# Attention and feed-forward on one core: the order of the two half-array scores after a row-maximum block

## The chip, the cores and the metric

The kernel runs on one core of a Trainium2 chip. The metric is device time of one execution in microseconds (us). The engines are named as in the profile: PE (TensorE matmuls), PEld (TensorE weight loads), DVE (VectorE), ACT (ScalarE), POOL (GpSimd) and SP (the queue that issues most DMAs).

## The reference

```python
def _attn_ref(q, k, v):                       # q, k, v: 4 x 8 heads x 1152 x 64
    factor = 2
    scale = 1.0 / np.sqrt(D)
    q_pool = q.reshape(B, H, S // factor, factor, D).mean(axis=3)
    scores = scale * np.matmul(q_pool, k.transpose(0, 1, 3, 2))
    scores = scores - np.max(scores, axis=-1, keepdims=True)
    attn = np.exp(scores)
    attn = attn / (np.sum(attn, axis=-1, keepdims=True) + 1e-09)
    return np.matmul(attn, v).astype(np.float32)

def _moe_ref(x, w_in, w_out, alpha):          # x: 2304 x 512, w_in: 512 x 2048
    h = x @ w_in
    g = np.maximum(h, 0.0) + alpha * np.minimum(h, 0.0)
    return (g @ w_out).astype(np.float32)
```

The attention output of all heads, laid side by side, is the x of the second function.

## The kernel before

The 32 heads are worked through in 16 pairs. A pair's two heads lie in the two halves of the 128 partitions, 64 dimensions each, so a matmul that contracts over one head's dimensions uses 64 rows of the array. The lower 64 rows are called tile 0 here and the upper 64 rows tile 1; a matmul on one can run beside a matmul on the other.

**Row maxima** (`pair_max`, `rows` at L818 and L825, `peaks` at L839). For a pair there are 28 row-maximum blocks, each of them for one head, so on one tile; in the list they alternate tile 0, tile 1. A block is one matmul of 384 columns (L818), or two of 288 columns (L825), into a PSUM bank, which DVE then reduces to a maximum for each row. The maxima reach the scores later as a fourth term (`mq`). The row maxima of pair n+1 are spread between the scores of pair n.

**Scores** (`half_main`, `scores` at L951). A pair has two halves of 288 query columns, and a half has 9 score blocks of 128 keys. A score block is 8 matmuls of 288 columns: four terms (high by high, high by low, low by high, and minus the maximum), each for tile 0 and then tile 1. Tile 0 accumulates in one PSUM bank and tile 1 in another. Two exponentials on ACT (L968) then read these banks, tile 0's first, and write `p`. In program order a block is tile 0, tile 1, tile 0, tile 1 and so on, whatever stood in front of it. I write S0 and S1 for the first score matmul of a block on tile 0 and on tile 1.

**The rest of a half.** POOL or DVE adds up the `p` tiles (L981); PE multiplies them by V (`weighted`, L995, 36 matmul records in a row for one half); the sums (L1017) give the denominators; DVE and ACT finish the rows (L1054 to L1066) and SP writes them to DRAM.

**Feed-forward** (L479). Low and high sweeps, three matmuls a product, use the whole array. From about 388 us on they are mixed into the last halves, and after 444 us PE does nothing else.

**What sets the order.** All of this is given to a planner (`Scheduler`) as tasks with priorities and estimated durations. It places one task after another on the engines and calls `emit` as it does so, and with that the order on each engine is fixed in the program. A score block is one task, and so is each exponential. PSUM banks are given out by the planner too. Each engine works its list from front to back and waits at semaphores.

Of the kernel before, what the change touches and what calls it, by code (L numbers as in the profile page):

```python
# [13 lines left out]
AF = mybir.ActivationFunctionType  # L14
# [15 lines left out]
class Buf:  # L30


    def __init__(self, ring=None):
        self.ring, self.t = ring, None
        self.writers, self.users = [], []
        if ring:
            ring.made.append(self)
# [71 lines left out]
class Scheduler:  # L109
# [3 lines left out]
    def __init__(self, col_cost, turn, to_pe, from_pe, slack, dma_fixed):  # L113
        self.tasks, self.ready = [], [[] for _ in range(5)]
        self.free = [0.0] * 5
        self.dma_free = 0.0
        self.now = 0.0
        self.col = 0
        self.lock_free = 0.0
        self.turn = turn  # L120
        self.col_cost, self.to_pe, self.from_pe, self.slack = col_cost, to_pe, from_pe, slack
        self.dma_fixed = dma_fixed
        self.hold = ()

    def add(self, eng, dur, emit, reads=(), writes=(), uses=(), deps=(), prio=0.0, col=0, size=0, kind=None, dma=False, lock=False, fixed=None):
        t = Task()
# [99 lines left out]
def attention_ffn(  # L226
# [87 lines left out]
    nc = tc.nc  # L314
# [6 lines left out]
    HQ = SQ // 2  # L321
# [6 lines left out]
    SCALE = 0.5 / float(D) ** 0.5  # L328

    def dve(n):  # L330
        return (n + 65) / 0.96

    def act(n, psum=False):
        return n / 1.2 + (50 if psum else 93)
# [14 lines left out]
    sch = Scheduler(COL, SF, TO_PE, FROM_PE, (SLP, SLA, SLD, 0, 0), DF)  # L349
# [285 lines left out]
    both = [slice(i * D, (i + 1) * D) for i in range(2)]  # L635
# [156 lines left out]
    def pair_max(n, w):  # L792
# [15 lines left out]
        for x, (t, j, i) in enumerate(items):  # L808
            ms, d = Buf(r_ms), both[i]
            p = n - M0 - 0.5 * MS * (len(items) - 1 - x)  # L810
            if first:
                p = -9 + 0.01 * x
            rest = t < 0
            m = S // 4 if rest else JW

            def rows(t=t, j=j, d=d, ms=ms):
                if t >= 0:
                    nc.tensor.matmul(  # L818
                        out=ms.t[:, :JW], lhsT=w.q1.t[d, starts[t]:starts[t] + P],
                        rhs=w.k1.t[d, j * JW:(j + 1) * JW], start=True, stop=True,  # L820
                    )
                    return
                for u in range(2):
                    c = (2 * j + u) * (S // 4)
                    nc.tensor.matmul(  # L825
                        out=ms.t[:, :S // 4], lhsT=w.rt.t[d, D - D * u:D - D * u + P],
                        rhs=w.k1.t[d, c:c + S // 4], start=u == 0, stop=u == 1,
                    )

            dur = 190 if rest else 130  # L830
            if first:
                deps = w.k_in if rest else [w.k_in[j], w.q_in[2 * (t > 1)]]
                add(PE, dur, rows, uses=[w.q1, w.k1], reads=[w.rt] if rest else (), deps=deps, writes=[ms], prio=p, kind="m", col=1)
            else:
                add(PE, dur, rows, reads=[w.rt if rest else w.q1, w.k1], writes=[ms], prio=p, kind="m", col=1)

            def peaks(t=t, j=j, i=i, ms=ms, m=m):
                at = i if t < 0 else 2 + t + i * (NQT - 1)
                nc.vector.tensor_reduce(out=bx.t[:, at, j:j + 1], in_=ms.t[:, :m], axis=AX.X, op=ALU.max)  # L839

            add(DVE, dve(m), peaks, reads=[ms], writes=[bx], prio=p)
            if first and x in (4 * NJ + 3, len(items) - 1):
                first_turn(x > 4 * NJ + 3, w, bx, mx, mq)
# [9 lines left out]
        def turn():  # L853
            for i, d in enumerate(both):
# [3 lines left out]
        t = [  # L858
            add(
                ACT, 110, lambda i=i, d=d: nc.scalar.activation(out=mm.t[:, d], in_=mt.t[i][:2 * NQT, :D], func=AF.Copy),  # L860
                reads=[mt], writes=[mm], prio=n - M0,
            )
            for i, d in enumerate(both)
        ]
# [3 lines left out]
                out=mm.t[:2, :D], in0=mt.t[1][:2, :D], in1=mm.t[:2, :D].bitcast(F32), op=ALU.max  # L868
# [3 lines left out]
        for i in range(2):  # L872
# [3 lines left out]
                    out=mq.t[i * D:i * D + 1, :REM].bitcast(F32).rearrange("o (t p) -> o t p", p=P),  # L876
                    in_=mm.t[2 + i * (NQT - 1):2 + (i + 1) * (NQT - 1)].bitcast(F32),
# [52 lines left out]
    def pair_main(n, w):  # L930
        for h in range(2):
            half_main(n, h, w)

    def half_main(n, h, w):
        late_head = n + h >= JH
        heads = [g[0] for g in PARTS[late_head]]
        ends = [g[-1] for g in PARTS[late_head]]
        acc[n + h], avs[n + h] = [], Buf(r_avs)
        av = Buf(r_av)
        t_acc, t_av, ps_ = None, None, []  # L940
        q = slice(h * HQ, (h + 1) * HQ)
        for c in range(NC):
            s = slice(c * P, (c + 1) * P)
            p, ps = Buf(r_p), Buf(r_ps)
            at = n + h + c / NC

            def scores(ps=ps, s=s):
                pairs = ((w.k1, w.q1), (w.k1, w.q2), (w.k2, w.q1), (None, w.mq))
                for x, (k, r) in enumerate(pairs):
                    for i, d in enumerate(both):  # L950
                        nc.tensor.matmul(  # L951
                            out=ps.t[i][:, :HQ], lhsT=k.t[d, s] if k else neg[d], rhs=r.t[d, q],
                            start=x == 0, stop=x == len(pairs) - 1,
                        )

            if n:
                add(PE, 545, scores, reads=[w.k1, w.q1, w.k2, w.q2, w.mq], writes=[ps], prio=at, kind="s", col=1)
            else:
                t = add(
                    PE, 545, scores, reads=[w.k1, w.q1, w.q2], uses=[w.k2, w.mq],  # L960
                    deps=w.k_low[:1 + (c >= 4)] + w.mq_in[0] + (w.mq_in[1] if h else []),
                    writes=[ps], prio=at, kind="s", col=1,
                )
                first_score.append(t)
            for i in range(2):
                add(
                    ACT, act(HQ, True),
                    lambda ps=ps, p=p, i=i: nc.scalar.activation(  # L968
                        out=p.t[:, i], in_=ps.t[i][:, :HQ], func=AF.Exp, scale=SCALE
                    ),  # L970
                    reads=[ps], writes=[p], prio=at + 0.01 * i,
                )
            if c in heads:

                part, t_acc, alone = p, None, True
            else:
                a, part = part, Buf(r_acc) if alone else part
                eng, dur, e = (DVE, dve(2 * HQ), nc.vector) if c in ADDS[late_head] else (POOL, 2.4 * 2 * HQ + 50, nc.gpsimd)
                t_acc = add(
                    eng, dur,  # L980
                    lambda a=a, b=p, part=part, e=e: e.tensor_tensor(out=part.t, in0=a.t, in1=b.t, op=ALU.add),  # L981
                    reads=[a, p], writes=[part], deps=[t_acc] if t_acc else [], prio=at, lock=True,
                )
                alone = False
            if c in ends:
                acc[n + h].append(part)
            ps_.append(p)
            if c not in GROUPS[late_head]:
                continue

            def weighted(c=c, ps_=ps_):
                for x, p in enumerate(ps_):
                    e = c - len(ps_) + 1 + x
                    for i in (1, 0):
                        nc.tensor.matmul(  # L995
                            out=av.t[i * D:(i + 1) * D, :HQ], lhsT=w.vv[i].t[:, e], rhs=p.t[:, i],
                            start=(e == 0), stop=(e == NC - 1),
                        )

            t_av = add(  # L1000
                PE, 486 * len(ps_), weighted, reads=w.vv + ps_, writes=[av],
                deps=[t_av] if t_av else [], prio=n + h + (c + GL) / NC, col=2,
            )
            ps_ = []
        add(
            ACT, act(HQ, True), lambda: nc.scalar.activation(out=avs[n + h].t, in_=av.t[:, :HQ], func=AF.Copy),
            reads=[av], writes=[avs[n + h]], prio=n + h + 1,
        )
# [70 lines left out]
    with ExitStack() as actx:  # L1079
# [64 lines left out]
        for n in range(0, NH, 2):  # L1144
# [4 lines left out]
        t = add(SP, 600, lambda: nc.sync.dma_start(out=nal, in_=alpha), uses=[], writes=[nal_b], deps=[first_load[0]], prio=3)  # L1149
# [3 lines left out]
                out=nal, in0=nal, scalar1=-1.0, scalar2=0.0, op0=ALU.mult, op1=ALU.add  # L1153
# [8 lines left out]
        for c in range(REUSE):  # L1162
            f, i = NLO + c // 2, c % 2
# [70 lines left out]
```

## Time and profile before

| what | value |
|---|---|
| device time, median of 3 runs | 840.44 us (839.09 to 842.27) |
| the profiled execution's own time | 839.95 us |
| span from its first to its last instruction | 838.2 us |
| PE busy | 825.2 us (98%) |
| DVE busy | 567.0 us (68%) |
| ACT busy | 437.4 us (52%) |
| mean granted TensorE clock | 0.999 |

A busy PE is not a PE at its peak: matmul records on the two tiles overlap, and a record is longer than the time until the next matmul on the same tile can start. A short wait between two matmuls therefore hides under the record of the one before.

### The profile page before, as it was taken

The numbers are of one execution on the slowest core, as the hardware profiler recorded it, in microseconds if no ns is written. First come the engines' busy times: TensorE is split into PE (matmuls) and PEld (weight loads), VectorE is DVE, ScalarE is ACT, GpSimd is POOL, SyncE is SP. The second block draws the span as 40 slices with busy tenths as digits, with TensorE's granted clock in tenths as the row PEclk, the third lists the DMA queues.
The fourth block names the chain that finished last, engine by engine and source line by source line (L and its number), as shares of the span: only waits on it lengthen the run. The fifth ranks groups of instructions, "written<-read, shape, count | busy, mean of one in ns | idle before, by whom it ended". The sixth has DMA issues, their size and how long they took to land.

```text
span 838.2 us, 17447 instructions
## 1 busy us (share of the span) xinstructions
PE 825.2 (98%) x6690; PEld 691.4 (82%) x6690; DVE 567.0 (68%) x1035; ACT 437.4 (52%) x1124; POOL 262.4 (31%) x196
## 2 busy tenths in 40 slices
PE   8999999999999999999999999999999999999997
PEld 8767777676777777776779999998898988988986
DVE  7999999999998988889963799632242232322422
ACT  4657676675766676665754676643232233332321
POOL 5665665565565665654550000000000000000000
PEclk9999999999999999999999999999999999999999
DMA  8234345634354433323233768581330421300301
GB/s 274 58 89 164 82 144 140 197 115 123 87 179 122 122 116 77 83 72 109 69 124 121 248 195 260 177 228 58 91 92 3 120 59 46 91 0 1 91 1 45
DMA packets 67759, 93.71 MB, mean 112 GB/s; under 512 B 20004, under 2 KB 45404, under 8 KB 67676
## 3 DMA queue, kind: packets, MB, share of 16 engines
q1 hardware_dynamic: 65516, 88.18, 33.9%
q0 software_dynamic: 2160, 4.42, 3.6%
q8 instruction: 52, 0.85, 0.4%
q14 instruction: 31, 0.25, 0.1%
HBM read 73.48 MB, written 19.02 MB: 110 GB/s over the span
## 4 chain that ended last, share of the span: by engine, by line
PE 86%; DVE 9%; DMA 2%; issue 1%; ACT 1%; SPq 0%; DVEq 0%; ACTq 0%
PE bank L479 44%; PE bank L951 18%; PE bank L995 15%; PE bank L818 6%; DVE bx L839 3%; PE bank L1017 2%; DMA wraw<-wt 1%; DVE x L1066 1%; DVE pa L981 1%; PE bank L825 1%; PE bank L1129 1%; DMA kk<-kt 1%; DVE pos L515 1%; DVE r L1054 0%; DVE wbits L415 0%
## 5 line engine op out<-in xcount | busy, mean ns | idle before, releaser
L981 POOL TENSOR_TENSOR pa<-pa,pa 128x576 f32<-128x576 f32 x160 | 240.5, 1520 | 155.9 <-ACT pa L968 104.4
L839 DVE TENSOR_REDUCE bx<-bank 128x1 f32<-128x384 f32 (+1 forms) x448 | 214.0, 533 | 22.5 <-PE bank L818 19.9
L968 ACT ACTIVATE pa<-bank 128x288 f32<-128x288 f32 x576 | 199.7, 417 | 25.9 <-PE bank L951 17.4
L951 PE MATMUL bank<-q,k 64*128 64x288 f32 x1728 | 206.2, 311 | 0.8 <-DVE mq L923 0.6
L951 PEld LDWEIGHTS bank<-q,k 64*128 64x128 f32 x1728 | 163.3, 184 | 21.1 <-issue 9.3
L995 PE MATMUL bank<-pa,vv 128*64 128x288 f32 x1152 | 146.8, 409 | 0.0
L995 PEld LDWEIGHTS bank<-pa,vv 128*64 128x64 f32 x1152 | 79.9, 137 | 54.8 <-issue 3.8
L526 DVE TENSOR_TENSOR gw<-gs,gw 128x460 fp32r<-128x460 f32 (+1 forms) x55 | 35.1, 638 | 121.2 <-ACT gw L521 121.2
L951 PE MATMUL bank<-mq,neg 64*128 64x288 f32 x576 | 115.2, 291 | 0.0
L818 PE MATMUL bank<-k,q 64*128 64x384 f32 x384 | 110.1, 362 | 3.5 <-DVE bx L839 2.0
L521 ACT ACTIVATE gw<-gs 128x460 fp32r<-128x460 f32 (+1 forms) x55 | 32.4, 589 | 126.7 <-PE bank L479 115.2
L479 PE MATMUL bank<-wlow,wh 128*128 128x460 f32 (+1 forms) x320 | 93.0, 371 | 0.0
L479 PE MATMUL bank<-gw,wh 128*128 128x460 f32 (+1 forms) x320 | 92.8, 371 | 0.0
L951 PEld LDWEIGHTS bank<-mq,neg 64*128 64x128 f32 x576 | 83.3, 184 | 0.0
L818 PEld LDWEIGHTS bank<-k,q 64*128 64x128 f32 x384 | 62.4, 185 | 16.2 <-DVE bx L839 10.0
L515 DVE SCALAR_TENSOR_TENSOR gs<-gs,nal 128x460 f32<-128x460 f32 (+1 forms) x55 | 38.4, 699 | 52.9 <-ACT gs L510 52.9
L479 PE MATMUL bank<-x,wlow 128*128 128x288 f32 x480 | 66.3, 296 | 0.0
L479 PEld LDWEIGHTS bank<-wlow,wh 128*128 128x128 f32 x320 | 60.0, 188 | 7.1
L479 PE MATMUL bank<-gs,wlow 128*128 128x288 f32 x480 | 65.8, 295 | 0.1
L479 PEld LDWEIGHTS bank<-gw,wh 128*128 128x128 f32 x320 | 60.1, 188 | 6.8
L479 PEld LDWEIGHTS bank<-x,wlow 128*128 128x128 f32 x480 | 64.2, 188 | 1.6 <-issue 1.4
L479 PEld LDWEIGHTS bank<-gs,wlow 128*128 128x128 f32 x480 | 63.9, 188 | 1.4 <-DVE gs L526 0.5
(90 smaller groups left out, 1006.2 us busy)
## 6 DMA issues: line engine op xcount, KB each, us to landing
wraw<-wt SPq DMA_DIRECT2D x32, 512.0 KB
vv<-vt SPq DMA_DIRECT2D x32, 288.0 KB
xs<-x SPq DMA_DIRECT2D x32, 288.0 KB
x<-xs SPq DMA_DIRECT2D x32, 288.0 KB
kk<-kt SPq DMA_DIRECT2D x15, 576.0 KB
r<-rrd SPq DMA_DIRECT2D x64, 72.0 KB
yp<-ys SPq DMA_DIRECT2D x32, 144.0 KB
wlow<-xs SPq DMA_DIRECT2D x16, 288.0 KB
```

Source lines behind the costliest of these rows:

```text
L479: nc.tensor.matmul(out=ps[:, :n], lhsT=w[a, c // DMO][:, c % DMO:c % DMO + P], rhs=lo(hl), start=(first and i == 0), stop=(last and i == 2),)
L515: lambda: nc.vector.scalar_tensor_tensor(out=flat(pos), in0=flat(neg), scalar=nal[:, f:f + 1], in1=flat(pos), op0=ALU.mult, op1=ALU.add),
L521: ACT, act(n), lambda: nc.scalar.activation(out=gs.t[:, 0, :n], in_=flat(pos), func=AF.Copy),
L526: lambda: nc.vector.tensor_tensor(out=gs.t[:, 1, :n], in0=flat(pos), in1=gs.t[:, 0, :n].bitcast(F32), op=ALU.subtract),
L818: nc.tensor.matmul(out=ms.t[:, :JW], lhsT=w.q1.t[d, starts[t]:starts[t] + P], rhs=w.k1.t[d, j * JW:(j + 1) * JW], start=True, stop=True,)
L825: nc.tensor.matmul(out=ms.t[:, :S // 4], lhsT=w.rt.t[d, D - D * u:D - D * u + P], rhs=w.k1.t[d, c:c + S // 4], start=u == 0, stop=u == 1,)
L839: nc.vector.tensor_reduce(out=bx.t[:, at, j:j + 1], in_=ms.t[:, :m], axis=AX.X, op=ALU.max)
L951: nc.tensor.matmul(out=ps.t[i][:, :HQ], lhsT=k.t[d, s] if k else neg[d], rhs=r.t[d, q], start=x == 0, stop=x == len(pairs) - 1,)
L968: lambda ps=ps, p=p, i=i: nc.scalar.activation(out=p.t[:, i], in_=ps.t[i][:, :HQ], func=AF.Exp, scale=SCALE),
L981: lambda a=a, b=p, part=part, e=e: e.tensor_tensor(out=part.t, in0=a.t, in1=b.t, op=ALU.add),
L995: nc.tensor.matmul(out=av.t[i * D:(i + 1) * D, :HQ], lhsT=w.vv[i].t[:, e], rhs=p.t[:, i], start=(e == 0), stop=(e == NC - 1),)
L1017: nc.tensor.matmul(out=ps.t[g * 32:(g + 1) * 32, :HQ], lhsT=ones, rhs=acc[n + g // 2][j].t[:, g % 2], start=j == 0, stop=j == m - 1, tile_ ...
```

## The change

The planner object keeps the tile that was used last (`tile`). A row-maximum block sets it to its own tile when it is emitted. A score block looks at it: if tile 0 was used last, its eight matmuls go tile 1, tile 0, tile 1, tile 0 and so on; otherwise they go as before. It then sets `tile` to the one it issued second. Its two exponentials take the tiles in the same order. Tasks, priorities, durations and the banks that the planner gives out are the same.

```diff
@@ Scheduler.__init__
         self.hold = ()
+        self.tile = 1
@@ pair_max
-            def rows(t=t, j=j, d=d, ms=ms):
+            def rows(t=t, j=j, d=d, ms=ms, i=i):
+                sch.tile = i
                 if t >= 0:
@@ half_main
-            def scores(ps=ps, s=s):
+            order = []
+
+            def scores(ps=ps, s=s, order=order):
                 pairs = ((w.k1, w.q1), (w.k1, w.q2), (w.k2, w.q1), (None, w.mq))
+                order.extend((1, 0) if sch.tile == 0 else (0, 1))
+                sch.tile = order[1]
                 for x, (k, r) in enumerate(pairs):
-                    for i, d in enumerate(both):
+                    for i in order:
+                        d = both[i]
                         nc.tensor.matmul(
@@ half_main, exponentials
-                    lambda ps=ps, p=p, i=i: nc.scalar.activation(
-                        out=p.t[:, i], in_=ps.t[i][:, :HQ], func=AF.Exp, scale=SCALE
+                    lambda ps=ps, p=p, o=order, i=i: nc.scalar.activation(
+                        out=p.t[:, o[i]], in_=ps.t[o[i]][:, :HQ], func=AF.Exp, scale=SCALE
                     ),
```

The order on DVE, POOL and SP is the same in both programs. On PE and ACT the instructions are the same in number and kind, and 112 of the 288 score blocks are turned round.

First place, PE before the change: the end of one score block, two row-maximum blocks (the first on tile 1, the second on tile 0), and the start of the next score block. In the scores, bank1 is tile 0's and bank4 tile 1's; in the block before them bank6 is tile 1's. A bracket names the engine that the instruction waits for.

```order
L951 MATMUL bank6_124<-mq0_111,neg_106 128x288
L818 MATMUL bank3_121<-k1_3359,q1_3340 128x384 [waits DVE_49]
L818 MATMUL bank0_118<-k1_3359,q1_3340 128x384 [waits DVE_49]
L951 MATMUL bank1_119<-q1_2602,k1_2645 128x288 [waits Activation_49]
L951 MATMUL bank4_122<-q1_2602,k1_2645 128x288 [waits Activation_49]
L951 MATMUL bank1_119<-q2_3040,k1_2645 128x288
L951 MATMUL bank4_122<-q2_3040,k1_2645 128x288
```

The same place on PE after the change:

```order
L958 MATMUL bank5_123<-mq0_111,neg_106 128x288
L820 MATMUL bank3_121<-k1_3359,q1_3340 128x384 [waits DVE_49]
L820 MATMUL bank0_118<-k1_3359,q1_3340 128x384 [waits DVE_49]
L958 MATMUL bank4_122<-q1_2602,k1_2645 128x288 [waits Activation_49]
L958 MATMUL bank1_119<-q1_2602,k1_2645 128x288
L958 MATMUL bank4_122<-q2_3040,k1_2645 128x288
L958 MATMUL bank1_119<-q2_3040,k1_2645 128x288
```

Tile 1's score has moved in front of tile 0's. Before, each of the two first scores had a wait for ACT of its own; after, only the one in front has one.

Second place, ACT before the change: the exponentials of three score blocks in a row. The third is the block whose start stands above; the first is the one that last used its two banks.

```order
L968 ACTIVATE pa2_90<-bank1_119 128x288 [waits PE_49]
L968 ACTIVATE pa2_90<-bank4_122 128x288 [waits PE_49]
L968 ACTIVATE pa3_91<-bank5_123 128x288 [waits PE_49]
L968 ACTIVATE pa3_91<-bank6_124 128x288 [waits PE_49]
L968 ACTIVATE pa4_92<-bank1_119 128x288 [waits PE_49,Pool_49]
L968 ACTIVATE pa4_92<-bank4_122 128x288 [waits PE_49]
```

The same six on ACT after the change:

```order
L975 ACTIVATE pa2_90<-bank1_119 128x288 [waits PE_49]
L975 ACTIVATE pa2_90<-bank4_122 128x288 [waits PE_49]
L975 ACTIVATE pa3_91<-bank6_124 128x288 [waits PE_49]
L975 ACTIVATE pa3_91<-bank5_123 128x288 [waits PE_49]
L975 ACTIVATE pa4_92<-bank4_122 128x288 [waits PE_49,Pool_49]
L975 ACTIVATE pa4_92<-bank1_119 128x288 [waits PE_49]
```

The first block keeps its order and the other two are turned round, so bank4, which the third block's scores now take first, is the bank that the first block's second exponential frees.

## Rows read from the trace of the kernel before

**Rows 1.** The page's head: span, then busy us, share and instructions by engine.

```profile
span 838.2 us, 17447 instructions
...
PE 825.2 (98%) x6690; PEld 691.4 (82%) x6690; DVE 567.0 (68%) x1035; ACT 437.4 (52%) x1124; POOL 262.4 (31%) x196
```

**Rows 2.** Busy us (and instructions) of each engine in stretches of 40 us.

```profile
core 0: us, PE busy (x) PEld busy (x) DVE busy (x) ACT busy (x) POOL busy (x), PEclk, DMA share, GB/s
60.00:100.00 40.00, 39.50 (x413) 30.31 (x409) 39.24 (x78) 27.07 (x74) 26.44 (x18) 1.00 0.34 103
140.00:180.00 40.00, 39.32 (x422) 29.45 (x420) 37.28 (x73) 28.14 (x76) 25.28 (x17) 1.00 0.47 145
...
300.00:340.00 40.00, 40.00 (x436) 30.27 (x434) 35.86 (x70) 27.62 (x76) 24.95 (x19) 1.00 0.40 120
```

**Rows 3.** Chain that ended last: start us, us, what; the 1st, 13th, 25th V product.

```profile
58.17 4.52 PE bank L995 x36
...
214.67 4.59 PE bank L995 x36
...
364.81 4.52 PE bank L995 x36
```

**Rows 4.** Whole program, PE's waits: us in total, times, longest us.

```profile
PE bank L951 <- ACT pa L968: 0.3, 1, 0.3
```

**Rows 5.** ACT's timeline, 247 to 251 us: start, us, what, xcount, idle before.

```profile
248.87 1.39 ACT L968 ACTIVATE pa<-bank 128x288 f32<-128x288 f32 x4
250.45 0.71 ACT L968 ACTIVATE pa<-bank 128x288 f32<-128x288 f32 x2 [0.20 <-PE bank L951]
```

**Rows 6.** ACT's timeline at 249.34 to 249.36 us: the second of those four alone.

```profile
249.16 0.48 ACT L968 ACTIVATE pa<-bank 128x288 f32<-128x288 f32 x1
```

**Rows 7.** PE's timeline from 248.2 us: four blocks, with row maxima (L818) between.

```profile
248.31 0.42 PE L951 MATMUL bank<-mq,neg 64*128 64x288 f32 x2
248.44 0.34 PE L818 MATMUL bank<-k,q 64*128 64x384 f32 x1
248.57 0.63 PE L951 MATMUL bank<-q,k 64*128 64x288 f32 x6
249.01 0.32 PE L951 MATMUL bank<-mq,neg 64*128 64x288 f32 x2
249.15 0.37 PE L818 MATMUL bank<-k,q 64*128 64x384 f32 x2
249.39 0.95 PE L951 MATMUL bank<-q,k 64*128 64x288 f32 x6
250.07 0.41 PE L951 MATMUL bank<-mq,neg 64*128 64x288 f32 x2
```

**Rows 8.** PE's timeline at 249.80 to 249.81 us: what is running then.

```profile
249.69 0.40 PE L951 MATMUL bank<-q,k 64*128 64x288 f32 x2
```

**Rows 9.** PE's timeline from 244.1 us: a block whose banks were both free.

```profile
244.61 0.67 PE L951 MATMUL bank<-q,k 64*128 64x288 f32 x6
245.12 0.29 PE L951 MATMUL bank<-mq,neg 64*128 64x288 f32 x2
```

**Rows 10.** ACT's waits for scores, 214 to 370 us: us in total, times, longest.

```profile
ACT pa L968 <- PE bank L951: 6.8, 30, 0.5
```

**Rows 11.** ACT's waits for scores, 0 to 214 us, in the same columns.

```profile
ACT pa L968 <- PE bank L951: 9.0, 31, 0.7
```

**Rows 12.** DVE's waits for row maxima, 214 to 370 us, in the same columns.

```profile
DVE bx L839 <- PE bank L818: 12.0, 12, 2.7
```

**Rows 13.** PE's timeline from 261.9 us: a block after one row maximum on tile 1.

```profile
264.00 0.29 PE L951 MATMUL bank<-mq,neg 64*128 64x288 f32 x1
264.12 0.34 PE L818 MATMUL bank<-k,q 64*128 64x384 f32 x1
...
264.70 0.29 PE L951 MATMUL bank<-mq,neg 64*128 64x288 f32 x1
```

**Rows 14.** PE's timeline from 437 us: the last half's end and the sweeps.

```profile
437.14 5.82 PE L479 MATMUL bank<-gs,wlow 128*128 128x288 f32 x42
442.89 1.18 PE L1017 MATMUL bank<-pa,ones 128*32 128x288 f32 x16
444.00 8.23 PE L479 MATMUL bank<-x,wlow 128*128 128x288 f32 x60
452.06 8.10 PE L479 MATMUL bank<-gs,wlow 128*128 128x288 f32 x60
```

## The prediction

> **What bounds the kernel now.** I read the page's head first: PE is busy for 825.2 of 838.2 us [rows 1], so the time is that of PE's list, and the question is where that list stands still without showing it. Then the stretches [rows 2]: early on DVE is nearly as full as PE (39.24 of 40 us from 60 to 100 us, 37.28 from 140 to 180), later less so (35.86 from 300 to 340). The chain of work that ended last gives the pace. The products with V, one for each half of a head pair, begin at 58.17, 214.67 and 364.81 us, 12 halves apart each time [rows 3]. So a half takes 156.5 / 12 = 13.0 us in the first stretch and 150.1 / 12 = 12.5 us in the second.
>
> The table of waits says that scores wait for exponentials for 0.3 us in the whole program [rows 4]. That is misleading: a matmul record of 0.29 to 0.40 us covers the gap behind it. The wait is seen by laying ACT's timeline beside PE's. Take one lap from a block's first exponential to that of the block two further on, which uses the same two banks. Four exponentials start at 248.87 [rows 5]; the second of them runs from 249.16 for 0.48 us, to 249.64 [rows 6]. PE has started S0 of the later block at 249.39 [rows 7]; S1 and the second matmul of tile 0 start together at 249.69 [rows 8], 0.05 us after that second exponential ended. The tile 0 chain ends with the matmul at 250.07 and tile 1's starts 0.12 us later, since the two make a row of 0.41 us where one takes 0.29 [rows 7, 9]. ACT, idle for 0.20 us, starts the later block's first exponential at 250.45, released by that tile 0 matmul [rows 5]. The lap is 250.45 - 248.87 = 1.58 us: 0.77 for two exponentials, 0.05 to S1, 0.38 from S1 to the last matmul of tile 0, and 0.38 from there to the exponential. **Scores and exponentials turn in a ring**: PE waits for the second exponential, ACT waits for the first score. Neither looks idle for long.
>
> **The change part by part.** *Nothing is added.* PE and ACT have the same instructions, and the lists of DVE, POOL and SP are the same, so no DMA moves. The adds (L981) and the product with V need both halves of `p` and see no difference in order. These edits cost nothing by themselves.
>
> *What is meant to be gained.* In 112 of 288 blocks the first score no longer stands behind a row maximum on its own tile. The price of standing there is about 0.13 us: one row maximum starts at 248.44 and the score behind it at 248.57 [rows 7]. But tile 0's matmul is still in the same list, now as the second one, and waits there for the same row maximum; what one tile gains the other has to make up before the block is complete. The trace of before has both cases already. After a single row maximum on tile 0 (same tile first), the last score row ends at 248.73 in one block and 249.33 in the next, 0.60 us [rows 7]. After a single one on tile 1 (free tile first, the case that the change makes general), the ends are 264.29 and 264.99, 0.70 us [rows 13]. The free tile first is not the shorter one. I take 0 for this gain, with 0.13 a block as its other end.
>
> *What it costs.* Before, every block went tile 0, tile 1, scores and exponentials alike. The bank that a block needs first was then the bank freed first, and the one it needs second was freed second. After, the order depends on the last row maximum, and with about three of them for two blocks it turns round every second block. The banks come back every second block too. In the order of the changed program, 161 blocks now begin with the bank that the *second* exponential of the block two earlier frees (none did before), and the ready one waits behind it in PE's list: only the first score has a wait for ACT. So both tiles start when S1 started before. How such a block runs is seen behind a product with V, where both banks had long been free: start 244.61, last two scores together at 245.12, 0.51 us later, in a row of 0.29 [rows 9]. The lap becomes 0.77 + 0.05 + 0.51 + 0.38 = 1.71 us in place of 1.58, so **0.13 us a lap**; one lap covers two blocks, as the ring of the odd and that of the even blocks turn side by side.
>
> The Trainium skill, page "TensorE: Matmul & The Clock Gate", Part 3, "What overlaps and what doesn't", says of matmuls "strict FIFO, no reordering". The trace agrees where tile 0's second matmul, free to go, starts only with S1 at 249.69 [rows 8]; by that rule the ready score is held as I assume, and without it the lap would not grow and the sum would be 0.
>
> *Where it is on the path.* From 214 to 370 us 76 of the turned-against blocks lie, 38 laps: 38 x 0.13 = 4.9 us if every lap is bound so. ACT visibly waits for a score 30 times there [rows 10]; at half a lap each that is 30 x 0.13 / 2 = 2.0 us, the lower bound. I take 30 x 0.13 = 3.9, nearer to the upper one, since in the lap I followed each part ends in the next one's start. Up to 214 us there are 77 blocks and 31 such waits [rows 11]: 77 / 2 x 0.13 = 5.0 us at most, 31 x 0.13 = 4.0 by the same reading. There DVE has 0.8 to 2.7 us of room in 40 [rows 2], so part of a delay on PE is time that PE would have waited for DVE anyway; I take half, 2.0, between 0 and 5.0. After 370 us 8 blocks are left: 8 / 2 x 0.13 = 0.5. If DVE's cover is gone, the first stretch pays its 4.0.
>
> The delay reaches the end unshortened: from 437 us on PE works without a gap, the last sums at 442.89 and the sweeps from 444.00 on [rows 14], and a list that is full to the end moves as a whole.
>
> Sum: 3.9 + 2.0 + 0.5 = 6.4 us, between 2.0 and 4.9 + 5.0 + 0.5 = 10.4. On the profiled execution's own 839.95 us, which is 0.5 us under the median of the runs (840.44), this is 846.4 us.
>
> **The rivals.** *The free tile pays (faster).* If the first score runs beside the row maximum and the second one loses nothing, 112 x 0.13 = 14.6 us go: 825.4 us; half of that, 832.7 us, if only every second one is on the path. For it: two row maxima and scores of the other tile do overlap [rows 13]. Against it: the 0.70 against 0.60 us above, and that the score then waits for a bank. It decides by whether the second exponential is over before the row maximum starts. The Trainium skill, page "TensorEngine Tiling (Array Packing)", "Key Properties", says that tiles operate independently, weight load and matmul in parallel; by that rule alone this rival would hold, and the trace has the overlap but not a shorter block.
>
> *Nothing to measure.* ACT has room in a half (27.62 of 40 us busy [rows 2]), and its waits sum to 6.8 us in 156 us [rows 10]. If a later first exponential is caught up by the next row of four, the lap ends as before: 840 to 842 us.
>
> *More than the ring (slower still).* The row maxima of the next pair stand between the scores. If they come late as well, DVE, which already waits 12.0 us for them from 214 to 370 us [rows 12], waits more in the stretch that it bounds, and all bounds are reached: 10.4 us and half as much again, 855 us.
>
> That the change doesn't turn the blocks is ruled out by the order of the two programs.
>
> **How the numbers follow.** Forecast, a ring that is longer by 2 to 10.4 us: 0.55. Nothing to measure: 0.25. Free tile pays: 0.12. Slower still: 0.08. A difference under 0.5%, 4.2 us, can hardly be told from none in this kernel, so "same" is 836.2 to 844.6 us: the second case with the lowest part of the forecast (0.03), 0.28. Slower: 0.52 + 0.08 = 0.60. Faster: 0.12. The range that holds 8 in 10 reaches from 839.5 us, which takes in no change, to 851 us, just above the forecast's upper bound of 850.4; the gain and the worst case are left out.
>
> **What the profile after would show.** If I am right: halves from 214 to 365 us at 12.8 to 12.9 us in place of 12.5; the first and the second score of a block starting together, 0.05 us after a second exponential; last score rows of 0.29 to 0.30 us in place of 0.41; more and longer idle time of ACT for scores than 30 times and 6.8 us; the same DVE time. If the free tile pays, the halves get shorter than 12.5 us and ACT's idle time shrinks. I would be wrong if a turned block's first score were seen to start before the second exponential of the block two earlier had ended, or if the halves kept 12.5 us with laps of 1.7 us, for then the ring is not what sets the pace.

## The result: slower by 1.1%

The changed kernel takes 849.94 us (median of 5 runs, 848.13 to 850.38), the kernel before 840.01 us (median of 5 runs, 839.09 to 842.27). The ratio is 1.011, with a 95% interval of 1.0093 to 1.0127. The profiled execution of the changed kernel took 849.94 us, with a span of 848.2 us; 10.0 us more than the span of before.

The page's head of the changed kernel, to be held against [rows 1]:

```profile
span 848.2 us, 17369 instructions
...
PE 831.0 (98%) x6690; PEld 685.1 (81%) x6690; DVE 570.4 (67%) x1035; ACT 434.3 (51%) x1124; POOL 259.6 (31%) x196
```

The same matmuls, reductions and exponentials, and PE again "busy" for 98% of a longer span. The head alone tells nothing of the cause.

The chain that ended last gives the pace; its columns are start us, us, what. The first, second and fourth of these rows answer to [rows 3]:

```profile
58.68 4.51 PE bank L1002 x36
...
219.24 4.59 PE bank L1002 x36
...
244.94 4.52 PE bank L1002 x36
...
372.67 4.52 PE bank L1002 x36
```

Read from [rows 3], the same products began at 58.17, 214.67 and 364.81 us. So 0.5 us is lost up to the first, 4.06 us between the first and the next that [rows 3] has, 3.29 us from there to the last one, and 10.0 - 7.86 = 2.1 us after it. From 219.24 to 372.67 us a half takes 153.43 / 12 = 12.8 us in place of 12.5.

The first 0.5 us may be chance: up to the same product (the 3rd of all), two profiles of one kernel differ by 0.6 to 0.7 us (runs 9 and 10).

Where it goes in a lap is seen at the very blocks that the prediction followed. ACT's timeline (start, us, what, idle before and what ended it):

```profile
253.64 1.38 ACT L975 ACTIVATE pa<-bank 128x288 f32<-128x288 f32 x4
255.36 1.32 ACT L975 ACTIVATE pa<-bank 128x288 f32<-128x288 f32 x4 [0.34 <-PE bank L958]
```

The same at 253.95 to 254.00 us, which leaves the first two of the four:

```profile
253.64 0.77 ACT L975 ACTIVATE pa<-bank 128x288 f32<-128x288 f32 x2
```

PE's timeline from 252.5 us, with row maxima at L820 and scores at L958:

```profile
253.20 0.29 PE L958 MATMUL bank<-mq,neg 64*128 64x288 f32 x2
253.33 0.34 PE L820 MATMUL bank<-k,q 64*128 64x384 f32 x1
253.34 0.73 PE L958 MATMUL bank<-q,k 64*128 64x288 f32 x6
253.81 0.39 PE L958 MATMUL bank<-mq,neg 64*128 64x288 f32 x2
253.95 0.43 PE L820 MATMUL bank<-k,q 64*128 64x384 f32 x2
...
254.97 0.30 PE L958 MATMUL bank<-mq,neg 64*128 64x288 f32 x2
```

PE's timeline at 254.60 to 254.61 us:

```profile
254.46 0.40 PE L958 MATMUL bank<-q,k 64*128 64x288 f32 x2
```

The first two exponentials end at 253.64 + 0.77 = 254.41. Both first scores of the block two further on start at 254.46, in one row of 0.40 us; before, tile 0's had started 0.30 us ahead of tile 1's [rows 7, 8]. The last two scores end together, a row of 0.30 us in place of 0.41 [rows 7]. ACT then waits 0.34 us in place of 0.20 [rows 5], and the lap is 255.36 - 253.64 = 1.72 us in place of 1.58.

The change does what it says, too: behind the single row maximum at 253.33 the score starts at 253.34, where it stood behind it for 0.13 us before [rows 7]. But from the end of the last score row to the end of the next one (253.49 to 254.20) this block takes 0.71 us, and it took 0.60.

ACT's waits for scores, 214 to 370 us in the first row and 0 to 214 us in the second (us in total, times, longest), answer to [rows 10] and [rows 11]:

```profile
ACT pa L975 <- PE bank L958: 11.9, 43, 0.4
...
ACT pa L975 <- PE bank L958: 14.1, 48, 0.6
```

11.9 us in place of 6.8 and 14.1 in place of 9.0. The other half of the ring, PE waiting for exponentials, is mostly hidden in PE's rows, but the weight loads ahead of the scores (PEld) note it. From 214 to 370 us, before and then after:

```profile
PEld bank L951 <- ACT pa L968: 0.2, 1, 0.2
```

```profile
PEld bank L958 <- ACT pa L975: 6.7, 27, 0.4
```

One wait has become 27. DVE waits for row maxima nearly as it did [rows 12], 12.9 us in two rows in place of 12.0 in one:

```profile
DVE bx L841 <- PE bank L820: 11.7, 8, 2.7
...
DVE bx L841 <- PE bank L827: 1.2, 5, 0.3
```

### The profile page after: what moved, and what is told of

It reads as the page before. It is cut to its first block, busy times and chain, and to the rows that moved or that the text cites. A ratio compares the mean times of both kernels' runs of the same rounds, so it can differ in the third digit from the quotient of the medians.

```text
span 848.2 us, 17369 instructions
## 1 busy us (share of the span) xinstructions
PE 831.0 (98%) x6690; PEld 685.1 (81%) x6690; DVE 570.4 (67%) x1035; ACT 434.3 (51%) x1124; POOL 259.6 (31%) x196
## 4 chain that ended last, share of the span: by engine, by line
PE 80%; DVE 10%; ACT 3%; DMA 3%; issue 2%; POOL 1%; SPq 0%; DVEq 0%; ACTq 0%; POOLq 0%
PE bank L480 41%; PE bank L958 17%; PE bank L1002 13%; PE bank L820 6%; DMA wraw<-wt 2%; DVE bx L841 2%; DVE pa L988 2%; PE bank L1024 2%; DVE x L1073 1%; ACT pa L975 1%; DVE wbits L416 1%; PE bank L827 1%; DVE pos L516 1%; DVE wbits L422 1%; PE bank L1136 1%
## 5 line engine op out<-in xcount | busy, mean ns | idle before, releaser
L988 POOL TENSOR_TENSOR pa<-pa,pa 128x576 f32<-128x576 f32 x160 | 237.7, 1501 | 168.6 <-ACT pa L975 116.8
L975 ACT ACTIVATE pa<-bank 128x288 f32<-128x288 f32 x576 | 197.1, 418 | 32.0 <-PE bank L958 28.9
L958 PE MATMUL bank<-q,k 64*128 64x288 f32 x1728 | 191.8, 311 | 3.6 <-ACT pa L975 1.5
L958 PEld LDWEIGHTS bank<-q,k 64*128 64x128 f32 x1728 | 139.9, 184 | 33.2 <-ACT pa L975 15.7
L820 PE MATMUL bank<-k,q 64*128 64x384 f32 x384 | 106.6, 360 | 4.0 <-DVE bx L841 1.7
L958 PE MATMUL bank<-mq,neg 64*128 64x288 f32 x576 | 98.2, 291 | 0.0
L820 PEld LDWEIGHTS bank<-k,q 64*128 64x128 f32 x384 | 59.3, 185 | 17.3 <-DVE bx L841 10.6
L958 PEld LDWEIGHTS bank<-mq,neg 64*128 64x128 f32 x576 | 67.1, 184 | 0.0
```

The costliest lines, as they stand in the source:

```text
L820: nc.tensor.matmul(out=ms.t[:, :JW], lhsT=w.q1.t[d, starts[t]:starts[t] + P], rhs=w.k1.t[d, j * JW:(j + 1) * JW], start=True, stop=True,)
L958: nc.tensor.matmul(out=ps.t[i][:, :HQ], lhsT=k.t[d, s] if k else neg[d], rhs=r.t[d, q], start=x == 0, stop=x == len(pairs) - 1,)
L975: lambda ps=ps, p=p, o=order, i=i: nc.scalar.activation(out=p.t[:, o[i]], in_=ps.t[o[i]][:, :HQ], func=AF.Exp, scale=SCALE),
```

## The experiments

**The theory:** a block now begins with the bank that the second exponential of the block two earlier frees, so the ring of scores and exponentials is longer. **Its rivals:** turning a block costs by itself; something beside the row maxima costs; and, for what was gained, that the free tile pays where the bank doesn't hide it. Products with V are counted over all 32. For each run the table has the us from the 5th to the 17th by PE's timeline, from the 17th to the 27th by its chain, and from there to the end of the span. "Against" is the number of blocks, by the program's order, that begin with the bank of a second exponential two blocks earlier. "PEld waits" are the weight loads for scores that wait for an exponential from 214 to 370 us, times and us in total, as in the two rows above.

| kernel | against | PEld waits | 5th to 17th | 17th to 27th | 27th to the end | median us | ratio to before, 95% |
|---|---|---|---|---|---|---|---|
| before | 0 | 1, 0.2 | 155.4 | 124.65 | 473.4 | 840.01 | |
| the change | 161 | 27, 6.7 | 159.6 | 127.73 | 475.5 | 849.94 | 1.0093 to 1.0127 |
| 1: turn every block | 1 | 1, 0.2 | 155.7 | 125.54 | 473.6 | 841.88 | 0.9998 to 1.0022 |
| 2: turn every two | 225 | 28, 6.9 | 160.2 | 127.87 | 474.2 | 849.95 | 1.0081 to 1.0128 |
| 3: banks to fit | 2 | none | 155.8 | 124.61 | 473.2 | 839.89 | 0.9972 to 0.9994 |
| 4: lead by one | 0 | none | 154.2 | 123.90 | 473.3 | 838.85 | 0.9963 to 0.9987 |
| 5: before, short reductions | 0 | 4, 0.8 | 153.7 | 123.39 | 472.3 | 835.78 | 0.9912 to 0.9953 |
| 6: after, short reductions | 161 | 37, 9.1 | 155.6 | 127.10 | 473.6 | 842.45 | 1.0005 to 1.0031 |
| 7: scores alone | 104 | 17, 4.0 | 156.2 | 126.30 | 473.3 | 843.01 | 1.0016 to 1.0039 |
| 8: banks to fit, lead by one | 2 | none | 154.5 | 122.84 | 472.9 | 836.67 | 0.9939 to 0.9974 |

The kernel before, run beside 1 to 4, took 840.94 us (median of 25), and beside 5 to 8 840.55 us (median of 24).

**1. Turn every block, whatever stood before it.**

```diff
-                order.extend((1, 0) if sch.tile == 0 else (0, 1))
-                sch.tile = order[1]
+                order.extend((1, 0) if sch.block % 2 else (0, 1))
+                sch.block += 1
```

> Every second score block is turned round (tile 1 first, exponentials too), whatever row maximum stood before it; 144 blocks are turned, more than the 112 of the change, but a block and the one two earlier have the same order, so only 1 block needs first a bank that the second exponential of the block two earlier frees (161 after the change). Ring of banks (my theory): no lap grows, 840 us, within 838.5 to 841.5. Rival, turning a block costs by itself (the array's upper half first, or the exponentials reversed): 9.9 us for 112 turned blocks, 144 x 9.9 / 112 = 12.7 us, 852.7 us.

Measured: 841.88 us, ratio 1.001 (0.9998 to 1.0022). Turning 144 blocks, tile 1 first and exponentials reversed, costs nothing in the whole that can be told from none; 12.7 us were expected if turning as such cost. It may cost a little: from the 17th to the 27th product the run takes 0.9 us more than before. Its chain:

```profile
240.21 4.52 PE bank L1003 x36
...
365.75 4.52 PE bank L1003 x36
```

**2. Turn every two blocks.** The same edit with `sch.block // 2 % 2`.

> The order turns round after every two score blocks, whatever row maximum stood before; 144 blocks are turned, as in the run that turns every block, but now 225 blocks need first the bank that the second exponential of the block two earlier frees. Ring of banks: 9.9 us for 161 such blocks gives 225 x 9.9 / 161 = 13.8 us, 854 us. Rival, turning costs by itself: the same time as the run that turns every block. Rival, the loss comes from what stands beside the row maxima: something else than both, since the rule no longer looks at them.

Measured: 849.95 us, 1.0105 (1.0081 to 1.0128). As many blocks are turned as in 1, no rule looks at row maxima, and the whole loss is there.

```profile
247.95 4.52 PE bank L1003 x36
...
375.82 4.52 PE bank L1003 x36
```

Runs 1 and 2 together settle it: the loss of the change is not the turning, nor the neighbourhood of the row maxima, but that a block's order differs from that of the block two earlier. The size was 854 us by my reckoning, and 849.95 is short of it: from the 17th to the 27th product 79 blocks against cost 3.2 us here, and 63 cost 3.1 us in the change. From 214 to 370 us the weight loads wait as often in both, 28 and 27 times, so by this count not every block against waits; why the further ones don't is open.

**3. The change, with the banks made to fit.** The rule stays; the tile that goes first takes the bank that was freed first.

```diff
                 sch.tile = order[1]
+                pair = frozenset(map(id, ps.t))
+                lead = sch.freed.get(pair, order[0])
+                if lead not in (id(ps.t[order[0]]), order[0]):
+                    ps.t = ps.t[::-1]
+                sch.freed[pair] = id(ps.t[order[0]])
```

> The change as it is (the free tile first, 112 blocks turned, the same order beside every row maximum), but the two banks of a block change places where needed, so that the tile issued first takes the bank that the first exponential frees; 2 blocks are left that need first a bank of a second exponential of two blocks earlier, in place of 161. Ring of banks: the loss is gone, 840 us, and whatever the free tile is worth is left alone to be seen: 0 by my reading, so 838.5 to 841.5. Rival, the loss is in turning or in the row maxima: 849.9 us. Rival, the free tile pays once the bank doesn't hide it: 840 less 7 to 14 us, 826 to 833.

Measured: 839.89 us, 0.9983 (0.9972 to 0.9994). One thing differs from the change, which PSUM bank belongs to which tile, and the loss is gone; so the bank is the cause. The waits of the weight loads for exponentials are gone from 214 to 370 us, too. What is left, 1.0 us between the medians, is what the free tile is worth, with whatever the turning costs taken off: something, but far from the 7 to 14 us of the rival.

```profile
240.13 4.52 PE bank L1008 x36
...
364.74 4.52 PE bank L1008 x36
```

**4. Tile 0 one matmul ahead, in the kernel before.** If the ring's length sets the pace, a shorter one should give time back.

```diff
-                for x, (k, r) in enumerate(pairs):
-                    for i, d in enumerate(both):
+                for x, i in ((0, 0), (1, 0), (0, 1), (2, 0), (1, 1), (3, 0), (2, 1), (3, 1)):
+                    (k, r), d = pairs[x], both[i]
```

> The kernel before, with tile 0 one matmul ahead of tile 1 in every score block: tile 0 twice, then 1, 0, 1, 0, 1, 1. While the first matmul of tile 1 waits for the second exponential, tile 0 has two matmuls done in place of one, so its last score ends one step of 0.13 us earlier after that wait. Ring of banks: the lap gets shorter by up to 0.13 us in up to 222 blocks; at the rate that the change measured (9.9 us for 161 blocks, 0.061 us a block) 13.7 us at most, so 826 to 836 us, with 834 as a middle since other bounds come near. Rival, the ring is not what sets the pace: 840 us. Rival, the uneven order makes the array idle where a row maximum stands between the blocks: over 842 us.

Measured: 838.85 us, 0.9975 (0.9963 to 0.9987), 2.1 us less where 4 to 14 were expected. ACT waits for scores 25 times for 5.7 us from 214 to 370 us, against 30 times and 6.8 us [rows 10]:

```profile
ACT pa L968 <- PE bank L951: 5.7, 25, 0.4
```

The direction is the ring's, the size is not. The lap that the prediction followed did get shorter, 250.53 - 249.06 = 1.47 us in place of 1.58 (ACT's timeline from 249.06 us and at 250.56 us):

```profile
249.06 1.39 ACT L968 ACTIVATE pa<-bank 128x288 f32<-128x288 f32 x4
```

```profile
250.53 0.41 ACT L968 ACTIVATE pa<-bank 128x288 f32<-128x288 f32 x1
```

The four exponentials in it take ACT 1.39 us, so little more is left to gain at such a place. A longer ring costs at once; a shorter one gives little, so in the kernel before something else is nearly as late: here ACT's own work, and runs 5 and 6 show another part.

**5 and 6. DVE's reductions cut to half their columns, in the kernel before and in the changed one.** What is subtracted is then the maximum over half the keys.

```diff
-                nc.vector.tensor_reduce(out=bx.t[:, at, j:j + 1], in_=ms.t[:, :m], axis=AX.X, op=ALU.max)
+                nc.vector.tensor_reduce(out=bx.t[:, at, j:j + 1], in_=ms.t[:, :m // 2], axis=AX.X, op=ALU.max)
```

> The kernel before, with DVE reducing only the first half of the columns of each row-maximum bank (192 of 384, 144 of 288), so what is subtracted is the maximum over half the keys; PE computes them all. It takes some 0.2 us from each of 448 reductions of 0.53 us, 90 us of DVE's work. If DVE bounded the first 240 us, as I took it in the prediction to cover half of the loss there, its 12 halves from the 5th to the 17th product with V (155.4 us before) come down by 3 to 8 us and the whole by as much: 832 to 837 us. If PE's list and the ring of banks set the pace there too and DVE's high busy share holds waits: 839 to 841.5 us, and the 155.4 us stay within 1.5.

> The changed kernel with the same half reductions on DVE (the maximum over half the keys is subtracted). If DVE covered part of the loss up to 240 us, then with its work cut the loss against the run of the kernel before with the same cut grows over 9.9 us, up to 12 or so. If DVE covered nothing: the same loss, 9 to 10.5 us above that run, and the 12 halves from the 5th to the 17th product with V stay 3.5 to 5 us longer than in it.

Measured: 835.78 and 842.45 us. The first shows how full DVE really was. Busy us in a stretch of 40 us, in the columns of [rows 2], of run 5:

```profile
60.00:100.00 40.00, 39.60 (x415) 30.12 (x411) 33.80 (x78) 26.76 (x74) 23.11 (x18) 1.00 0.34 103
```

DVE falls from 39.24 to 33.80 us of 40, and yet the first stretch gets only a little faster: in its chain the 17th product starts at 238.11 in place of 240.16, and the 27th 123.39 us later in place of 124.65.

```profile
84.36 4.52 PE bank L995 x36
...
238.11 4.52 PE bank L995 x36
...
361.50 4.51 PE bank L995 x36
```

From the 5th product to the 17th it is 153.75 us where the second profile of before, below, has 240.75 - 85.46 = 155.29: 1.5 us less (1.7 against the first profile). That is about the 1.5 us of the case in which DVE bounds nothing, while the whole, 835.78 us, lies in the range of the other: neither expectation held as a whole. DVE bounds these halves a little, and no more in the first stretch than in the second. The chain of run 6, and its 5th product in PE's timeline:

```profile
242.12 4.52 PE bank L1002 x36
...
369.22 4.52 PE bank L1002 x36
```

```profile
86.48 4.59 PE L1002 MATMUL bank<-pa,vv 128*64 128x288 f32 x36
```

With the work of DVE cut, the change still loses 242.12 - 238.11 = 4.0 us up to the 17th product, against 244.94 - 240.16 = 4.8 without the cut. But 2.2 of these 4.0 us are lost in the start-up, before the 3rd product (at 60.56 and 58.34 us by PE's timeline). From the 5th to the 17th the loss is 155.57 - 153.74 = 1.8 us, against 159.62 - 155.44 = 4.2 without the cut, and from there to the 27th 127.10 - 123.39 = 3.7 us, against 3.1. So DVE did not cover the loss in the first stretch: taking its load away does not make the loss larger there. It makes it smaller, and that was in neither expectation (3.5 to 5 us if DVE covered nothing, more if it did). Why the same blocks cost less there with DVE relieved is open. Between the medians of the two runs the loss is 6.7 us, where 9 or more were expected; the profiled execution of run 6, 844.59 us, was the slowest of its ten.

**7. The scores turned, the exponentials as before.**

```diff
-                    lambda ps=ps, p=p, o=order, i=i: nc.scalar.activation(
-                        out=p.t[:, o[i]], in_=ps.t[o[i]][:, :HQ], func=AF.Exp, scale=SCALE
+                    lambda ps=ps, p=p, i=i: nc.scalar.activation(
+                        out=p.t[:, i], in_=ps.t[i][:, :HQ], func=AF.Exp, scale=SCALE
```

> Half of the change: the scores are turned by its rule, the exponentials stay tile 0 first. Turned blocks (112) then first need the bank that the second exponential frees, and the others none: 104 such blocks two apart in place of 161. Ring of banks: 9.9 x 104 / 161 = 6.4 us, 847 us (845 to 848.5); a turned block's first exponential waits for its second score, but both end together there, so nothing more. Rival, the reversed exponentials are what costs: 840 us. Rival, the turned scores cost alone, whatever the exponentials do: 850 us.

Measured: 843.01 us, 1.0027 (1.0016 to 1.0039); 847 was expected, 845 at the least. Both rivals, 840 and 850, fail too. From the 17th to the 27th product the loss follows the count in these two: 34 blocks against cost 126.30 - 124.65 = 1.65 us, 0.049 us each, and the change's 63 cost 3.08 us, 0.049 us each (run 2's 79 cost less each). Up to the 17th it does not: 66 blocks cost 240.90 - 240.16 = 0.7 us, where the change's 90 cost 4.8. That stretch takes a small number of longer laps almost for free and a larger one at full price; why is not settled. The other half of the change, the reversed exponentials alone, was not run.

```profile
240.90 4.52 PE bank L1002 x36
...
367.20 4.52 PE bank L1002 x36
```

**8. Banks to fit and lead by one, together.** The edits of 3 and 4, with the lead given to the tile that goes first.

> The free tile first with the two banks changed round to fit, and the tile issued first one matmul ahead of the other. If the small gains of the two runs (0.17% and 0.25%) come from different places, they add: 837 to 838 us. If both take the same wait, the score behind a row maximum or behind the second exponential: 838.5 to 839.5 us. If the lead of one matmul makes the second tile's last score late where a row maximum stands on it: 840 us or more.

Measured: 836.67 us, 0.9956 (0.9939 to 0.9974), faster than both kernels. The gains of 3 and 4 (0.17% and 0.25%) add up, within the intervals.

```profile
238.32 4.52 PE bank L1008 x36
...
361.16 4.52 PE bank L1008 x36
```

ACT's waits for scores from 214 to 370 us are down to 21 and 4.8 us:

```profile
ACT pa L981 <- PE bank L964: 4.8, 21, 0.3
```

**9 and 10. Both kernels once more.**

> The changed kernel once more, for a second profile of it. In the first one the steps between products with V were 159.6 us (5th to 17th), 158.7 us (17th to 29th) and 38.9 us (29th to 32nd), against 155.4, 155.2 and 37.3 before. If the 1.6 us of the last step belong to the change, they are seen again; if they are chance in the order of events where the feed-forward loads its weights, the step is near 37.4 us, as in the runs with every second and every two blocks turned. The first two steps stay within 0.7 us if they are the ring's.

> The kernel before once more, for a second profile: the steps 155.4, 155.2 and 37.3 us should come again within 0.7 us, and 17th to 29th within 0.5. What they differ by is the noise of such a step in one profile.

Measured: 850.26 and 840.12 us, one execution each. The changed kernel's chain:

```profile
85.95 4.52 PE bank L1002 x36
...
245.57 4.52 PE bank L1002 x36
...
404.36 4.52 PE bank L1002 x36
...
441.74 4.52 PE bank L1002 x36
```

And the kernel before's:

```profile
85.46 4.52 PE bank L995 x36
...
240.75 4.52 PE bank L995 x36
...
396.00 4.51 PE bank L995 x36
...
433.37 4.52 PE bank L995 x36
```

The steps are 159.62, 158.79 and 37.38 us after, and 155.29, 155.25 and 37.37 us before: the first two steps repeat within 0.2 us, and the third is not longer by the change. What the first profile of the changed kernel lost there, 1.6 us, is lost elsewhere in the second. Its span is 848.5 us, so 406.8 us follow on 441.74, and 405.0 follow on 433.37 before. PE's waits from 400 us to the end, of the first profile of the changed kernel and then of the second:

```profile
PE bank L958 <- ACT rs L1036: 1.2, 1, 1.2
```

```profile
PE bank L480 <- DVE gs L527: 0.7, 1, 0.7
```

In one it is a score that waits for ACT to read the sums, in the other a sweep that waits for DVE; the kernel before has no PE wait in that stretch in either profile. These waits are 1.2 and 0.7 us, less than what is lost. No run here takes this loss of 1.6 to 1.7 us by itself, and its cause stays open.

## Why the prediction was right, step by step

**The mechanism, right.** That PE's few noted waits hide a ring was read from three narrow rows [rows 6 to 8], and runs 1, 2 and 3 show it: more turning without the mismatch, no loss clear of noise; mismatch without the rule, the loss; the rule with banks to fit, no loss. The weight loads' waits for exponentials go the same way: 1, 28 and none, against 27 in the change.

**The price of a lap, right.** 0.13 us was worked out from a block behind a product with V [rows 9]; the same lap is 1.72 us after and 1.58 before, 0.14 us. 161 blocks are 80 laps, and 80 x 0.13 is the upper bound of 10.4 us; the medians differ by 9.9. That these two come so near is in part luck: the 9.9 us hold the 1.6 to 1.7 us at the end that no lap accounts for, and run 2 loses no more with 225 such blocks.

**The gain of the free tile, taken as 0: nearly right.** Run 3 puts it at 0.17% (0.06% to 0.28%), 1.0 us between the medians, whatever turning costs taken off.

**214 to 370 us: 3.9 us predicted, 3.3 measured.** The bounds were 2.0 and 4.9.

**Up to 214 us: 2.0 us predicted, 4.6 measured.** This is the term that was mis-sized. I halved 4.0 because DVE was busy for 37 to 39 of 40 us, and took a busy share for a bound. Run 5 takes away about 5 of 40 us of that work and a half gains only 0.1 us; run 6 shows that it hid none of the loss. Without the halving the term is 4.0 and the sum 8.4. That 4.0 comes so near is no proof of the 31 laps behind it: with DVE's work cut, run 6 loses 1.8 us from the 5th to the 17th product where the change loses 4.2, so DVE's load makes the loss dearer there, by a way that no run shows.

**After 370 us: 0.5 us predicted, 2.1 measured.** The 8 blocks are there: from the 27th to the 29th product the second profiles give 404.36 - 373.35 = 31.0 us after and 396.00 - 365.38 = 30.6 before, 0.4 us. The rest, 1.7 us, is what moved between two profiles, and its cause is open.

**"The list that is full to the end moves as a whole"** held for the sweeps, apart from those 1.7 us.

**The rivals.** "Nothing to measure" fell by the result; "the free tile pays" by the result and by run 3; "more than the ring" needed all bounds to be passed and DVE to wait longer for row maxima: from 214 to 370 us the loss stays under its bound of 4.9, and DVE waits 12.9 us, both rows taken together, where it waited 12.0 [rows 12].

The rule "strict FIFO, no reordering" of the Trainium skill (page "TensorE: Matmul & The Clock Gate", Part 3, "What overlaps and what doesn't") agrees with the row at 254.46, where the ready tile starts only with the one that waited. It does not hold for every start: in the kernel before, a score on tile 0 starts at 224.67 us, 0.13 us ahead of the row maximum that stands in front of it in the program, on the other tile and with no wait noted:

```profile
224.67 0.29 PE L951 MATMUL bank<-q,k 64*128 64x288 f32 x1
224.80 0.33 PE L818 MATMUL bank<-k,q 64*128 64x384 f32 x1
```

So what held the ready score back at 254.46 reads as the wait in front of it, and not its place in the list alone.

## What to carry to other kernels

Two buffers that an engine fills and another empties are freed in the order in which they were emptied; whoever turns round the order of filling must turn round which buffer goes with it, or the first one waits for the last one freed. A busy share near 100%, of PE or of DVE, is not yet a bound: ask which row's end starts the next row, and cut the work once to see. Where the matmul rows hide a wait, look at the weight loads. Look for a ring by following one buffer from release to release; its length and the pace of the loop must agree before a stage is called bound by it.

## What the runs showed that I had not expected

A ring that is the pace in one direction is not so in the other: 0.13 us more a lap cost 9.9 us, and run 4's head start of one step for tile 0 gave back 2.1 us. In the kernel before no single thing that was eased gave as much as 1%: cutting DVE gave 0.7%, the lead 0.25%, the free tile 0.17%, and lead and free tile together 0.44%.

DVE's busy time seems to hold waits as PE's does, and a mean hides which. The same 24 adds (L981 before, L988 after) between the 3rd and the 15th product with V take 844 ns in the mean before and 909 after, with no idle time noted in front. The least, the median and the longest in ns, before and then after:

```profile
L981 DVE TENSOR_TENSOR pa<-pa,pa x24: 684/746/1961, 58.0 to 204.6; 128x576 f32<-128x576 f32 x24
```

```profile
L988 DVE TENSOR_TENSOR pa<-pa,pa x24: 735/747/2224, 58.5 to 209.1; 128x576 f32<-128x576 f32 x24
```

The median is the same. Two adds before and three after take 1.95 us or more, and each of them starts while an add of POOL is running and ends 0.6 us after it, as here before the change:

```profile
60.24 1.59 POOL L981 TENSOR_TENSOR pa<-pa,pa 128x576 f32<-128x576 f32 x1
...
60.49 1.96 DVE L981 TENSOR_TENSOR pa<-pa,pa 128x576 f32<-128x576 f32 x1
```

That reads as DVE held up until POOL is done, but no run takes it by itself. It is not the loss of the change either: run 3, which loses nothing, has the same mean of 909 ns.
